# The weights' rounding on GpSimd, row sums ended once per pair, and three units' activations rounded on ScalarE

## The chip, the core and the metric

The kernel runs on one core of one Trainium2 chip. The metric is device time in microseconds: the median before is 724.19 us over three runs (723.75 to 724.37). Five engines work on the core, each through its own instructions in order: TensorE (PE, with its weight loads as PEld), VectorE (DVE), ScalarE (ACT), GpSimd (POOL) and SyncE (SP, which issues nearly all transfers). Semaphores tie them together.

## The reference

Sliding-window attention with a few sink tokens, whose output goes through a two-layer network with a clipped activation:

```
scores = q @ k.T / sqrt(64)              # 4 batches, 8 heads, 768 tokens, 64 wide
keep   = (pos_k < 4) | ((0 <= i - j) & (i - j < 128))
a      = softmax(where(keep, scores, -1e9))
x      = (a @ v) as 3072 tokens x 512
h      = x @ w_in                        # 512 x 2048, float64 in memory
g      = h * clip(h + 3, 0, 6) / 6
out    = g @ w_out                       # 2048 x 512, float64 in memory
```

## The kernel before

A unit is 256 tokens of one batch; there are 12 (3 for each of 4 batches). The four units that begin a batch come first, then the other eight. For each unit the attention runs in 4 pairs of heads, so there are 48 pairs, `s` = 0 to 47. Pairs 0 to 9 are plain (`plain(s)`): they see no earlier tokens and use unsplit float32 products. Two heads of a pair and two blocks of 128 tokens give four score blocks.

For one plain pair the steps are: scores on PE (`sp`, L309), masked minimum on DVE (L316), exponential on ACT with a row sum into `sm` (L338), for each head on DVE a sum plus 1e-9 (L340) and a reciprocal `rc` (L341), the division of each block by its row sum (`norm`: token block 0 on DVE at L326, block 1 on ACT at L324), transposes on PE (`pt`, L364), a copy to SBUF on ACT (`pf`, L35), the product with V on PE (`av`, L431), and the split of the result into a rounded high part `xh` (ACT, L35) and a low part `xl` (DVE, L447).

The network works in 8 slices `i` of 256 hidden columns (`ffn1`, `ffn2`), each product in three terms of high and low parts. For a unit and a slice PE writes `hps` (L472, 24 products of 256 columns), ACT makes relu(h + 3) in `gf` (L484), DVE clips and multiplies (L485), then `gf` is rounded to `gh` (L41, on DVE) and DVE subtracts to get `g` (L487). PE then runs 12 products of 512 columns (L498), one slice later in units 0 and 1 and two later from unit 2 on.

The weights come as float64 and are turned into a rounded high and a low part once, slice by slice: `wih0` and `wil0`, `woh0` and `wol0`, `wih1` and so on, 16 parts of 128 x 1024. Each part (`load_part`) is a transfer into `st`, an ACT pass into `wt` (L157), an ACT pass on `st` (L161), two DVE passes (L163, L165) that end in the float32 value in `wt`, a rounding copy to the high part (ACT, L35) and a DVE subtraction for the low part (L168). Three buffers serve `st` and two serve `wt`, so a part can only start when an older one is through. The parts are asked for in pairs 2 to 10, one to three per pair (`WN`).

What each engine does next is fixed at build time. The code is written as a software pipeline (`ORDER`), in which a pair's scores, its softmax and its product with V stand in three successive rounds and steps of the network fill the places between them, and a scheduler then sets each engine's order. In pairs 0 to 3 PE also runs products whose result nobody uses (`idle`, L81). The letters in `WHI`, `GHI` and the like choose the engine: D is DVE, A is ACT, P is POOL. `eng(which, s)` takes the letters after the first for units 0 to 2 (it is called with 4 times the unit's number, and `START` is 9) and the first letter from unit 3 on.

Of the kernel before, what the change touches and what calls it, by code (L numbers as in the profile page):

```python
# [14 lines left out]
ALU = mybir.AluOpType  # L15
# [3 lines left out]
P = 128  # L19
# [7 lines left out]
def split_parts(nc, hi, lo, src, hi_engine, lo_engine):  # L27

    copy_r(nc, hi_engine, hi, src)
    lo_engine.tensor_tensor(out=lo, in0=src, in1=hi.bitcast(F32), op=ALU.subtract)  # L30


def copy_r(nc, eng, out, src, scale=1.0):
    if eng is nc.scalar:
        nc.scalar.mul(out=out, in_=src, mul=scale)  # L35
    elif eng is nc.gpsimd:
        nc.gpsimd.tensor_scalar(out=out, in0=src, scalar1=scale, scalar2=1.0, op0=ALU.mult, op1=ALU.mult)
    elif scale != 1.0:
        nc.vector.tensor_scalar(out=out, in0=src, scalar1=scale, scalar2=None, op0=ALU.mult)
    else:  # L40
        nc.vector.tensor_copy(out=out, in_=src)  # L41
# [3 lines left out]
def attn_ffn_kernel(ctx: ExitStack, tc: tile.TileContext, qx, kx, vx, vfx, vsx, n_sink, window, w_in, w_out, out):  # L45
    nc = tc.nc
# [3 lines left out]
    H, D, UT = 2 * NP, 64, 256  # L50
# [26 lines left out]
    def keep_busy(n):  # L77

        idle = ps.tile([P, 512], F32, tag="bank", name="idle")
        for _ in range(n):  # L80
# [15 lines left out]
                                   op0=ALU.mult, op1=ALU.add)  # L96
# [30 lines left out]
    WOH = [const.tile([P, 2, DM], F32R, name=f"woh{i}") for i in range(NFP)]  # L127
    WOL = [const.tile([P, 2, DM], F32R, name=f"wol{i}") for i in range(NFP)]
    wide = mybir.dt.size(w_in.dtype) == 8
    WHI, WLO = "A", "D"  # L130

    def weng(which, at):
        return {"D": nc.vector, "P": nc.gpsimd, "A": nc.scalar}[which[at % len(which)]]
# [5 lines left out]
    def load_part(hi, lo, src, rows, at):  # L139

        def like(t):
            return t.rearrange("p (a b) -> p a b", a=rows)

        st = work.tile([P, PW, 2], I32, tag=("sb0", "sb1", "K")[at % 3 if at < LAST else at % 2], name="st", bufs=1)
        if not wide:
            st = like(st.rearrange("p n w -> p (n w)").bitcast(F32)[:, 0:PW])
            nc.sync.dma_start(out=st, in_=src)
            split_parts(nc, hi, lo, st, nc.scalar, nc.vector)
            return

        it = work.tile([P, PW], I32, tag=("w0", "kt")[at % 2 if at < LAST else 0], name="wt", bufs=1)
        nc.sync.dma_start(out=like(st.rearrange("p n w -> p (n w)")), in_=src.bitcast(I32))
        low, high = st[:, :, 0], st[:, :, 1]
        ft = it.bitcast(F32)


        nc.scalar.activation(out=ft, in_=high.bitcast(F32), func=AF.Abs, scale=2.0 ** -112)  # L157

        nc.scalar.activation(out=low, in_=low.bitcast(U32), func=AF.Copy, scale=2.0 ** -29 * (1 - 2.0 ** -18),  # L161
                             bias=7.5 * 2.0 ** -18 - 0.5)
        nc.vector.scalar_tensor_tensor(out=low, in0=high, scalar=-2 ** 31, in1=low,  # L163
                                       op0=ALU.bitwise_and, op1=ALU.bitwise_or)
        nc.vector.scalar_tensor_tensor(out=it, in0=it, scalar=3, in1=low,  # L165
                                       op0=ALU.logical_shift_left, op1=ALU.bitwise_or)
        copy_r(nc, weng(WHI, at), hi, like(ft))
        weng(WLO, at).tensor_tensor(out=lo, in0=like(ft), in1=hi.bitcast(F32), op=ALU.subtract)  # L168
# [31 lines left out]

    SSE = "DD"
    START = 9
    GHI, GLO = "DD", "DD"
    XHI, XLO = "DDA", "DD"
    KHI, KLO, QHI, QLO = "AA", "DD", "AA", "DD"

# [18 lines left out]
    def plain(s):  # L225
        return s < NF32 and pus[s][1] == 0
# [62 lines left out]
    def cell(s, h, t, c0, c1):  # L289

        if plain(s):
            return st_[s][f"P{h}"][:, t * P + c0:t * P + c1]
        return st_[s]["P"][:, h, t * WP + c0:t * WP + c1]
# [26 lines left out]
    NORM0, NORM = "DADA", "AAAA"  # L320

    def norm(e, blk, c):
        if e == "A":
            nc.scalar.mul(out=blk, in_=blk, mul=c)  # L324
        elif e == "D":
            nc.vector.tensor_scalar(out=blk, in0=blk, scalar1=c, scalar2=None, op0=ALU.mult)  # L326
        else:
            nc.gpsimd.tensor_scalar(out=blk, in0=blk, scalar1=c, scalar2=1.0, op0=ALU.mult, op1=ALU.mult)

    def C_soft(s, h):  # L330
        b, u, p = pus[s]
        d = st_[s]
        nb, sm, rc = d["nb"], d["sm"], d["rc"]
        hs = slice(2 * h, 2 * h + 2)
        live = [(0, W2), (0, W2)] if u else [(0, P), (0, 2 * P)]
        for t in range(2):
            i, blk = 2 * h + t, cell(s, h, t, *live[t])
            d["exp"] = nc.scalar.activation(out=blk, in_=blk, func=AF.Exp, scale=-1.0,  # L338
                                            bias=nb[:, i:i + 1], accum_out=sm[:, i:i + 1])
        nc.vector.tensor_scalar(out=sm[:, hs], in0=sm[:, hs], scalar1=1e-9, scalar2=None, op0=ALU.add)  # L340
        nc.vector.reciprocal(out=rc[:, hs], in_=sm[:, hs])  # L341
        if u:

            both = d["P"][:, h].rearrange("p (t w) -> p t w", t=2)[:, :, P:2 * P]
            prior = d["P"][:, h, 0:2 * WP].rearrange("p (t w) -> p t w", t=2)[:, :, 0:P]
            nc.gpsimd.tensor_tensor(out=both, in0=both, in1=prior, op=ALU.add)  # L346
            live = [(P, W2), (P, W2)]
        for t in range(2):
            i, blk = 2 * h + t, cell(s, h, t, *live[t])
            norm((NORM0 if s < START else NORM)[i], blk, rc[:, i:i + 1])  # L350
        if u and h == 1:

            ss = ssc.rearrange("p (t k h y) -> p t k h y", t=2, k=2, h=2)
            snk_in = d["P"][:, :, 2 * P:2 * WP].rearrange(
                "p h (t y) -> p t h y", t=2)[:, :, :, 0:SK]
            split_parts(nc, ss[:, :, 0], ss[:, :, 1], snk_in, weng(SSE, 0), weng(SSE, 1))

    def D_pt(s, h):
        b, u, p = pus[s]
        d = st_[s]  # L360
        blocks = ((0, P), (1, P + SK)) if u else ((0, 0), (1, 0), (1, P))
        pt = ps.tile([P, 512], F32, tag="bank", name="pt")
        for j, (t, c) in enumerate(blocks):
            nc.tensor.transpose(out=pt[:, j * P:(j + 1) * P], in_=cell(s, h, t, c, c + P), identity=ident)  # L364
        w = P * len(blocks)
        if plain(s):
            ph = work.tile([P, 512], F32, tag="ph", name="pf")
            copy_r(nc, {"D": nc.vector, "A": nc.scalar}[PFE[h]], ph[:, 0:w], pt[:, 0:w])
            d[f"pt{h}"] = ph
            return  # L370
        ph = work.tile([P, 512], F32R, name="ph")
        pl = work.tile([P, 512], F32R, name="pl")
        d[f"pt{h}"] = (ph, pl)
        if not u:
            split_parts(nc, ph[:, 0:w], pl[:, 0:w], pt[:, 0:w], nc.scalar, nc.vector)
            return


        own, prior = ([x.rearrange("p (t s q) -> p t s q", t=2, s=2)[:, :, i, :] for x in (ph, pl)] for i in (1, 0))
        split_parts(nc, own[0], own[1], pt[:, 0:w].rearrange("p (t q) -> p t q", t=2), nc.scalar, nc.vector)  # L380
        for i in range(2):
            nc.gpsimd.affine_select(out=prior[i], in_=own[i], pattern=[[0, 2], [-1, P]], base=0,  # L382
                                    channel_multiplier=1, compare_op=ALU.is_gt, fill=0.0)
            nc.gpsimd.affine_select(out=own[i], in_=own[i], pattern=[[0, 2], [1, P]], base=0,
                                    channel_multiplier=-1, compare_op=ALU.is_ge, fill=0.0)
# [174 lines left out]
    def slot_C(s, h, t):  # L560
        if 0 <= s < NS:
            C_score(s, h, t)
            if t == 1:
                C_soft(s, h)
                if s == 0 and h == 1:
                    keep_busy(WARM[1])
                elif 0 < s < NP:
                    keep_busy(WARM[2])
# [62 lines left out]
    with tc.If(flag == 1):  # L631
        with ExitStack() as gen:
# [71 lines left out]
            with tc.For_i(0, B, 1) as bi:  # L704
                for u in range(NU):
                    xn = gp.tile([P, NP, UT], F32, name="xn")
                    for c in range(NP):
                        nc.sync.dma_start(out=xn[:, c, :],
                                          in_=xv[ds(bi, 1), :, c, u * UT:(u + 1) * UT].rearrange("o p s -> (o p) s"))
# [75 lines left out]
```

## Time and profile before

| | |
|---|---|
| median of 3 runs | 724.19 us |
| the profiled execution: its time, and the span of its records | 723.47 us, 721.8 us |
| PE busy | 706.4 us, 98% |
| DVE busy | 497.0 us, 69% |
| ACT busy | 420.6 us, 58% |
| POOL busy | 173.2 us, 24% |
| TensorE clock granted, mean over the span | 0.994 |

The span is what the records cover; the run's own time is 1.7 us longer. PE counts as busy while a product is in its pipeline, so short gaps between products are hidden in "busy". An idle stretch is put down to the instruction that ended it. The shares are means over stages that differ much: the first 110 us, in which the weights are prepared, look unlike the rest.

### The profile page before, as it was taken

What the parts mean: (1) busy time and instruction counts of PE and PEld (TensorE: products, weight loads), DVE (VectorE), ACT (ScalarE), POOL (GpSimd) and SP (SyncE); (2) the same over time, 40 slices, a digit from 0 to 9 for tenths busy, and PEclk for the clock granted to TensorE, in tenths of its full rate; (3) what the DMA queues carried; (4) which work ended last, traced back from release to release, by engine and by line L of the source; (5) the groups of instructions that cost most, each with busy time, mean ns of one, the idle gap of its engine ahead of it and who ended that gap; (6) DMA issues with size and microseconds to landing.
All of it is one profiled execution on the core that took longest, in us unless ns stands there. A gap on an engine that the chain in (4) does not pass through costs nothing. (4 is left out here: it accounts for less than half of the span.)

```text
span 721.8 us, 14212 instructions
## 1 busy us (share of the span) xinstructions
PE 706.4 (98%) x4772; PEld 638.3 (88%) x4772; DVE 497.0 (69%) x1370; ACT 420.6 (58%) x1091; POOL 173.2 (24%) x336
## 2 busy tenths in 40 slices
PE   9898899999999999999999999999999999999996
PEld 7776788999999999999998998999999999998985
DVE  5799888657676776777777777777777677543331
ACT  5999777556566556566566665655665665411211
POOL 1000000000035334325334434343334335200000
PEclk9999899999999999999999999999999999999999
DMA  7667555344454454555544544553644632000000
GB/s 290 201 209 242 189 173 156 89 103 134 109 139 132 126 134 132 135 139 137 138 118 118 161 115 115 136 147 90 182 119 109 170 93 61 30 1 1 30 1 34
DMA packets 53296, 89.10 MB, mean 123 GB/s; under 512 B 8160, under 2 KB 38112, under 8 KB 51168
## 3 DMA queue, kind: packets, MB, share of 16 engines
q1 hardware_dynamic: 53072, 88.11, 43.6%
q8 instruction: 40, 0.66, 0.4%
q14 instruction: 40, 0.33, 0.2%
q10 hardware_dynamic: 144, 0.00, 0.0%
HBM read 42.47 MB, written 6.29 MB: 68 GB/s over the span
## 5 line engine op out<-in xcount | busy, mean ns | idle before, releaser
L472 PE MATMUL hps<-xh,wih 128*128 128x256 f32 x768 | 220.7, 287 | 4.0 <-ACT wih L35 4.0
L472 PE MATMUL hps<-xh,wil 128*128 128x256 f32 x768 | 218.0, 284 | 0.7 <-DVE wil L168 0.7
L472 PE MATMUL hps<-xl,wih 128*128 128x256 f32 x768 | 217.0, 282 | 1.2 <-DVE xl L447 1.2
L498 PE MATMUL o<-woh,gh 128*128 128x512 f32 x384 | 155.0, 404 | 0.6 <-DVE gh L41 0.6
L472 PEld LDWEIGHTS hps<-xh,wih 128*128 128x128 f32 x768 | 145.6, 190 | 7.3 <-ACT wih L35 5.3
L498 PE MATMUL o<-wol,gh 128*128 128x512 f32 x384 | 151.7, 395 | 0.0
L498 PE MATMUL o<-woh,g 128*128 128x512 f32 x384 | 151.5, 395 | 0.0
L472 PEld LDWEIGHTS hps<-xl,wih 128*128 128x128 f32 x768 | 145.7, 190 | 2.4 <-DVE xl L447 1.4
L472 PEld LDWEIGHTS hps<-xh,wil 128*128 128x128 f32 x768 | 145.6, 190 | 1.7 <-DVE wil L168 1.1
L485 DVE SCALAR_TENSOR_TENSOR gf<-gf,hps 128x512 f32<-128x512 f32 x96 | 65.8, 685 | 83.1 <-ACT gf L484 82.2
L346 POOL TENSOR_TENSOR Pt<-Pt 128x256 f32<-128x256 f32 x64 | 47.4, 741 | 295.8 <-ACT Pt L338 295.7
L338 ACT ACTIVATE Pt<-Pt,nb 128x272 f32<-128x272 f32 (+2 forms) x152 | 77.0, 507 | 66.8 <-DVE nb L316 65.9
L484 ACT ACTIVATE gf<-hps,three 128x512 f32<-128x512 f32 x96 | 66.0, 687 | 81.9 <-PE hps L472 80.9
L324 ACT ACTIVATE Pt<-Pt,rc 128x144 f32<-128x144 f32 (+2 forms) x152 | 55.7, 414 | 65.3 <-DVE rc L341 41.8
L498 PEld LDWEIGHTS o<-woh,g 128*128 128x128 f32 x384 | 72.2, 188 | 16.7
L498 PEld LDWEIGHTS o<-woh,gh 128*128 128x128 f32 x384 | 72.4, 189 | 11.0 <-DVE gh L41 1.0
L498 PEld LDWEIGHTS o<-wol,gh 128*128 128x128 f32 x384 | 72.5, 189 | 10.0
L487 DVE TENSOR_TENSOR g<-gf,gh 128x512 fp32r<-128x512 f32 x96 | 69.7, 726 | 0.7
L316 DVE CUSTOM_DVE_ANT_0 Pt<-sp,m_t 128x272 f32<-128x272 f32 x128 | 54.0, 429 | 12.0 <-PE sp L314 10.7
L314 PE MATMUL sp<-K 128*128 128x272 f32 (+2 forms) x304 | 60.7, 285 | 0.0
L382 POOL TENSOR_SCALAR_AFFINE_SELECT ph<-ph 128x256 fp32r<-128x256 f32 x64 | 30.8, 480 | 119.0 <-ACT ph L35 119.0
L314 PEld LDWEIGHTS sp<-K 128*128 128x128 f32 x304 | 51.2, 188 | 6.4
(96 smaller groups left out, 1086.3 us busy)
## 6 DMA issues: line engine op xcount, KB each, us to landing
K<-kt SPq DMA_DIRECT2D x128, 200.0 KB, 3.5
K<-kt SPq DMA_DIRECT2D x152, 64.0 KB, 2.1
st<-in_w_in_dram SPq DMA_DIRECT2D x8, 1024.0 KB, 5.3
st<-in_w_out_dram SPq DMA_DIRECT2D x8, 1024.0 KB, 5.0
kr<-in_kx_dram SPq DMA_DIRECT2D x32, 200.0 KB, 2.4
qr<-in_qx_dram SPq DMA_DIRECT2D x48, 128.0 KB, 2.3
out_dram<-ost SPq DMA_DIRECT2D x24, 256.0 KB, 2.4
vr<-in_vx_dram SPq DMA_DIRECT2D x32, 192.0 KB, 2.5
```

The costliest lines, as they stand in the source:

```text
L314: nc.tensor.matmul(out=sp[:, 0:w], lhsT=Q[:, h, t * P:(t + 1) * P], rhs=K[:, h, part, k0c:k0c + w], start=(part == 0), stop=(part == 1))
L316: d["min"] = nc.vector.tensor_tensor_reduce(out=cell(s, h, t, 0, w), in0=sp[:, 0:w], in1=m[:, 0:w], scale=-SCALE, scalar=3.0e38, op0=ALU.a ...
L324: nc.scalar.mul(out=blk, in_=blk, mul=c)
L338: d["exp"] = nc.scalar.activation(out=blk, in_=blk, func=AF.Exp, scale=-1.0, bias=nb[:, i:i + 1], accum_out=sm[:, i:i + 1])
L346: nc.gpsimd.tensor_tensor(out=both, in0=both, in1=prior, op=ALU.add)
L382: nc.gpsimd.affine_select(out=prior[i], in_=own[i], pattern=[[0, 2], [-1, P]], base=0, channel_multiplier=1, compare_op=ALU.is_gt, fill=0.0)
L472: nc.tensor.matmul(out=hp[:, half, :], lhsT=l, rhs=r, start=(j == 0), stop=(j == n - 1))
L484: nc.scalar.activation(out=gf, in_=hp, func=AF.Relu, bias=three, scale=1.0)
L485: nc.vector.scalar_tensor_tensor(out=gf, in0=gf, scalar=6.0, in1=hp, op0=ALU.min, op1=ALU.mult)
L487: eng(GLO, state["n"] * NP).tensor_tensor(out=g, in0=gf, in1=gh.bitcast(F32), op=ALU.subtract)
L498: nc.tensor.matmul(out=acc, lhsT=l[:, f, ts_], rhs=r[i][:, f, :], start=(i == 0 and f == 0 and j == 0), stop=(i == NFP - 1 and f == 1 and ...
```

## The change

`WHI` becomes "P": the rounding of all 16 weight parts moves from ACT to POOL, and `copy_r` uses a plain copy there in place of a multiplication by two scalars. `GHI` becomes "DA": for units 0, 1 and 2 the rounding of `gf` to `gh`, 24 instructions, moves from DVE to ACT. In plain pairs (0 to 9) the sum plus 1e-9 and the reciprocal are done once for both heads on four columns, after the second head's exponentials, and the divisions of both heads follow.

```
@@ copy_r
     elif eng is nc.gpsimd:
-        nc.gpsimd.tensor_scalar(out=out, in0=src, scalar1=scale, scalar2=1.0, op0=ALU.mult, op1=ALU.mult)
+        nc.gpsimd.tensor_copy(out=out, in_=src)
@@ attn_ffn_kernel
-    WHI, WLO = "A", "D"
+    WHI, WLO = "P", "D"
...
-    GHI, GLO = "DD", "DD"
+    GHI, GLO = "DA", "DD"
@@ C_soft, behind the exponentials of head h
+        heads = [h]
+        if plain(s):
+            if h == 0:
+                return
+            heads, hs = [0, 1], slice(0, 4)
         nc.vector.tensor_scalar(out=sm[:, hs], in0=sm[:, hs], scalar1=1e-9, scalar2=None, op0=ALU.add)
         nc.vector.reciprocal(out=rc[:, hs], in_=sm[:, hs])
...
-        for t in range(2):
-            i, blk = 2 * h + t, cell(s, h, t, *live[t])
-            norm((NORM0 if s < START else NORM)[i], blk, rc[:, i:i + 1])
+        for g in heads:
+            for t in range(2):
+                i, blk = 2 * g + t, cell(s, g, t, *live[t])
+                norm((NORM0 if s < START else NORM)[i], blk, rc[:, i:i + 1])
```

The scheduler builds a new order on PE, DVE and ACT for the first 110 us or so. Six lines are added ahead of most of the code, so a line of after is 6 higher from L351 on and L340, L341 become L345, L346. Three places follow.

First place, DVE around slice 1 and the low part `wil1` (the numbers behind names are buffers; `wt_509` of before is `wt_499` of after). Before:

```order
L163 SCALAR_TENSOR_TENSOR st_508<-st_508 128x1024
L165 SCALAR_TENSOR_TENSOR wt_509<-wt_509,st_508 128x1024
L168 TENSOR_TENSOR wil1_120<-wt_500,wih1_112 128x1024
L485 SCALAR_TENSOR_TENSOR gf_531<-gf_531,hps_486 128x512
L168 TENSOR_TENSOR wol1_136<-wt_509,woh1_128 128x1024
L41 CAST gh_530<-gf_531 128x512
```

After:

```order
L168 TENSOR_TENSOR wil1_120<-wt_490,wih1_112 128x1024
L326 TENSOR_SCALAR Ph_439<-Ph_439,rc_438 128x128
L326 TENSOR_SCALAR Ph_448<-Ph_448,rc_438 128x128
L165 SCALAR_TENSOR_TENSOR wt_499<-wt_499,st_498 128x1024
L163 SCALAR_TENSOR_TENSOR st_626<-st_626 128x1024
L168 TENSOR_TENSOR wol1_136<-wt_499,woh1_128 128x1024
L491 SCALAR_TENSOR_TENSOR gf_521<-gf_521,hps_476 128x512
L165 SCALAR_TENSOR_TENSOR wt_627<-wt_627,st_626 128x1024
L493 TENSOR_TENSOR g_519<-gf_521,gh_520 128x512
```

`wil1` moved ahead of the last pass on `woh1`, only one pass now stands between that pass and `wol1`, which reads POOL's rounding, and `gf` stands behind `wol1`.

Second place, DVE around `wol4` and `wil5`. Before:

```order
L165 SCALAR_TENSOR_TENSOR wt_884<-wt_884,st_883 128x1024
L163 SCALAR_TENSOR_TENSOR st_892<-st_892 128x1024
L163 SCALAR_TENSOR_TENSOR st_1045<-st_1045 128x1024
L168 TENSOR_TENSOR wol4_139<-wt_884,woh4_131 128x1024
L165 SCALAR_TENSOR_TENSOR wt_893<-wt_893,st_892 128x1024
```

After:

```order
L326 TENSOR_SCALAR Ph_830<-Ph_830,rc_814 128x128
L165 SCALAR_TENSOR_TENSOR wt_868<-wt_868,st_867 128x1024
L165 SCALAR_TENSOR_TENSOR wt_877<-wt_877,st_876 128x1024
L168 TENSOR_TENSOR wol4_139<-wt_868,woh4_131 128x1024
L168 TENSOR_TENSOR wil5_124<-wt_877,wih5_116 128x1024
L491 SCALAR_TENSOR_TENSOR gf_918<-gf_918,hps_885 128x512
```

Two last passes and the two low parts that need POOL's roundings now stand in a row.

Third place, ACT between slice 3's `gf` of unit 0 and the copies that follow. Before:

```order
L484 ACTIVATE gf_807<-hps_774,three_75 128x512
L161 ACTIVATE st_883<-st_883 128x1024
L324 ACTIVATE Ph_829<-Ph_829,rc_828 128x256
L338 ACTIVATE Ph_848,sm_827<-Ph_848,nb_826 128x256
L35 ACTIVATE xh2_870<-av_861 128x256
L35 ACTIVATE wih4_115<-wt_875 128x1024
```

After:

```order
L490 ACTIVATE gf_793<-hps_760,three_75 128x512
L324 ACTIVATE Ph_699<-Ph_699,rc_698 128x256
L324 ACTIVATE Ph_714<-Ph_714,rc_698 128x256
L161 ACTIVATE st_867<-st_867 128x1024
L35 ACTIVATE pf_777<-pt_773 128x384
L35 ACTIVATE pf_802<-pt_798 128x384
L157 ACTIVATE wt_868<-st_867 128x1024
L35 ACTIVATE gh_792<-gf_793 128x512
```

The rounding of `wih4` is gone from ACT, and the new rounding `gh_792` stands six instructions behind its `gf`.

## Rows read from the trace of the kernel before

**Rows 1.** Busy time by stretch of the span: length, then busy us (and instructions) of PE, PEld, DVE, ACT and POOL, the granted clock, the DMA share and GB/s.

```profile
30.00:40.00 10.00, 7.84 (x52) 6.30 (x52) 8.96 (x25) 9.94 (x22) 0.00 (x0) 1.00 0.79 263
40.00:80.00 40.00, 36.32 (x212) 28.75 (x212) 38.68 (x80) 36.88 (x68) 0.00 (x0) 1.00 0.68 230
80.00:90.00 10.00, 8.38 (x35) 7.24 (x36) 8.19 (x21) 7.23 (x15) 0.00 (x0) 0.66 0.39 134
90.00:110.00 20.00, 20.00 (x129) 17.33 (x127) 16.96 (x34) 16.21 (x32) 0.00 (x0) 1.00 0.52 165
110.00:200.00 90.00, 90.00 (x616) 82.08 (x615) 61.88 (x188) 57.28 (x153) 1.47 (x2) 1.00 0.46 121
200.00:650.00 450.00, 450.00 (x3152) 414.39 (x3151) 324.01 (x921) 261.88 (x737) 168.62 (x318) 1.00 0.46 119
```

**Rows 2.** All waits of PE over the span: who waited for whom, us in total, times, the longest.

```profile
PE hps L472 <- ACT wih L35: 4.0, 3, 2.1
PE pt L364 <- DVE Ph L326: 1.6, 1, 1.6
PE idle L81 <- POOL rel L65: 1.2, 1, 1.2
PE hps L472 <- DVE xl L447: 1.2, 1, 1.2
PE hps L472 <- DVE wil L168: 0.7, 1, 0.7
PE o L498 <- DVE gh L41: 0.6, 1, 0.6
```

**Rows 3.** Busy time by stretch again, behind the wait for slice 5; the granted clock is the third number from the end.

```profile
81.00:82.00 1.00, 0.39 (x2) 0.30 (x2) 1.00 (x5) 1.00 (x4) 0.00 (x0) 0.94 0.54 82
82.00:85.00 3.00, 3.00 (x9) 2.03 (x9) 3.00 (x9) 3.00 (x7) 0.00 (x0) 0.50 0.87 334
85.00:88.00 3.00, 3.00 (x16) 3.00 (x16) 3.00 (x8) 1.55 (x3) 0.00 (x0) 0.50 0.25 81
88.00:89.00 1.00, 1.00 (x7) 1.00 (x7) 0.19 (x1) 0.00 (x0) 0.00 (x0) 0.65 0.00 0
```

**Rows 4.** Groups of instructions of the first 130 us by line, engine and shape: count, busy us and mean ns of one, idle time before them.

```profile
L165 DVE SCALAR_TENSOR_TENSOR wt<-wt,st 128x1024 int32<-128x1024 int32 x16 | 19.5, 1217 | 0.1
...
L168 DVE TENSOR_TENSOR wol<-wt,woh 128x1024 fp32r<-128x1024 f32 x8 | 9.8, 1222 | 0.6 <-ACT woh L35 0.6
...
L35 ACT ACTIVATE woh<-wt 128x1024 fp32r<-128x1024 f32 x8 | 8.5, 1063 | 0.5 <-DVE wt L165 0.5
L35 ACT ACTIVATE wih<-wt 128x1024 fp32r<-128x1024 f32 x8 | 8.4, 1052 | 0.2 <-DVE wt L165 0.2
...
L487 DVE TENSOR_TENSOR g<-gf,gh 128x512 fp32r<-128x512 f32 x11 | 7.5, 683 | 0.0
...
L41 DVE CAST gh<-gf 128x512 fp32r<-128x512 f32 x11 | 4.6, 421 | 0.7 <-PE o L498 0.7
...
L340 DVE TENSOR_SCALAR sm<-sm 128x2 f32<-128x2 f32 x23 | 3.5, 163 | 0.4 <-ACT Ph L338 0.2
L341 DVE RECIPROCAL rc<-sm 128x2 f32<-128x2 f32 x23 | 3.4, 157 | 0.2
...
L35 ACT ACTIVATE vs<-raw_s 128x512 fp32r<-128x512 f32 x2 | 1.2, 620 | 0.0
```

**Rows 5.** The same view for POOL over the whole span: the copies, and a two-input instruction.

```profile
L346 POOL TENSOR_TENSOR Pt<-Pt 128x256 f32<-128x256 f32 x64 | 47.4, 741 | 295.8 <-ACT Pt L338 295.7
...
L72 POOL CAST ident_r<-ident 128x128 fp32r<-128x128 f32 x1 | 0.3, 292 | 0.1
...
L188 POOL COPY m_t<-m_t 128x16 bf16<-128x16 bf16 x1 | 0.2, 196 | 0.0
```

**Rows 6.** Timeline of DVE at 194 and 291 us: start us, us, instruction; a number in brackets is the idle time before it.

```profile
194.42 0.99 DVE L41 CAST gh<-gf 128x512 fp32r<-128x512 f32 x1
...
291.39 0.43 DVE L41 CAST gh<-gf 128x512 fp32r<-128x512 f32 x1
...
291.85 1.25 DVE L487 TENSOR_TENSOR g<-gf,gh 128x512 fp32r<-128x512 f32 x1
```

**Rows 7.** Timeline of POOL at the same two places.

```profile
194.40 0.73 POOL L346 TENSOR_TENSOR Pt<-Pt 128x256 f32<-128x256 f32 x1 [185.76 <-ACT Pt L338]
...
291.82 0.74 POOL L346 TENSOR_TENSOR Pt<-Pt 128x256 f32<-128x256 f32 x1 [3.13 <-ACT Pt L338]
```

**Rows 8.** Timeline of DVE at the low parts of slices 1 and 5, and behind the latter.

```profile
39.79 1.22 DVE L168 TENSOR_TENSOR wil<-wt,wih 128x1024 fp32r<-128x1024 f32 x1
...
81.59 1.23 DVE L168 TENSOR_TENSOR wil<-wt,wih 128x1024 fp32r<-128x1024 f32 x1
...
90.04 0.69 DVE L485 SCALAR_TENSOR_TENSOR gf<-gf,hps 128x512 f32<-128x512 f32 x1 [1.85 <-ACT gf L484]
...
92.05 0.42 DVE L447 TENSOR_TENSOR xl<-av,xh 128x256 fp32r<-128x256 f32 x1 [0.79 <-ACT xh L35]
```

**Rows 9.** All waits of DVE between 40 and 82 us.

```profile
DVE wol L168 <- ACT woh L35: 0.6, 2, 0.3
DVE gf L485 <- ACT gf L484: 0.3, 1, 0.3
DVE Ph L316 <- PE sp L309: 0.2, 1, 0.2
```

## The prediction, made before the run

> **What bounds the kernel now.** I read the time by stretches first. From 110 us on PE is busy without a gap (90.00 of 90, 450.00 of 450), DVE and ACT have a quarter to two fifths of their time free [rows 1]. Nothing that only makes an engine lighter there can move the end; time can be won or lost only as long as PE waits, in the first 110 us. There the picture is turned round: between 40 and 80 us DVE is busy 38.68 of 40 us and ACT 36.88 of 40, while PE shows gaps [rows 1]. Both are preparing weights. POOL does nothing in that time.
>
> The list of PE's waits says what those gaps are worth: three waits for a high part of w_in, 4.0 us; one each for a normalised block, 1.6, for `xl`, 1.2, for `wil`, 0.7, for `gh`, 0.6 [rows 2]. (The 1.2 us for `rel` is the program's start.) That is 8.1 us. Beside the waits stands the clock: it falls to 0.50 (1.2 GHz in place of 2.4) at about 82 us, right behind PE's longest wait of 2.1 us, and is back before 89 [rows 2, 3]. The stretch from 80 to 90 us has a mean of 0.66 [rows 1], so 3.4 us of work at full speed are lost. 8.1 + 3.4 = 11.5 us is what a faster preparation could give at the very most.
>
> The question is therefore what the change does to the pace of DVE, the fuller of the two, from the first weight to the last. In the ledger below I count from the low part of slice 1 (39.79 us) to that of slice 5 (81.59) [rows 8], 41.8 us in which DVE waits only 1.1 us [rows 9]. The sum is made against the profiled run (723.47 us with a span of 721.8); it lies 0.7 us under the median of 724.19, and I put the difference that comes out on the median.
>
> **Prices.** A high part on ACT is 1.05 to 1.06 us [rows 4]; 16 of them, 16.9 us, leave ACT. On POOL no copy of that size is in the trace. Its CAST of 128 columns takes 292 ns and its COPY of 16 columns 196 ns [rows 5]: 0.86 ns a column, so 292 + 896 x 0.86 = 1.06 us by this estimate. The upper bound is the two-input instruction, 741 ns for 256 columns [rows 5], 2.96 us for 1024; I take 1.06, since the CAST is the same operation, and a copy has one input. `gh` on ACT is priced by the nearest copy of 128x512, 620 ns [rows 4]; on DVE it took 421 [rows 4]. One sum and one reciprocal fewer per plain pair is 163 + 157 = 0.32 us of DVE [rows 4].
>
> **Term 1, up to the first slices: -1.4 us.** Three roundings (`wih0`, `woh0`, `wih1`) leave ACT ahead of the first network steps, at most 3.2 us. Against that, a block of head 0 is now normalised only when head 1's exponentials are through. In the order of ACT a weight pass (L157 or L161) mostly stands in that place, so it costs little. Bounds: -3.2, all of ACT's time on the path, and +1.6, PE's one wait for a normalised block [rows 2] a second time. I take -1.4, a little on the side of the gain, because three of the first four pairs have such a pass there. PE's waits for a normalised block and `xl` (2.8 us together) are those that it can shorten.
>
> **Term 2, slice 1 to slice 5: +1.1 us.** Removed from DVE: four `gh`, 4 x 0.42 = 1.7; three pairs' ends, 3 x 0.32 = 1.0; the waits of 1.1 us, nearly all for ACT, 1.0. Added: DVE and POOL collide. Alone, `g` takes 683 ns; where POOL had begun a tensor-tensor 0.03 us before it, it took 1.25 us, and `gh`, 421 ns alone, took 0.99 [rows 4, 6, 7]. Both ended 0.28 to 0.54 us after POOL did, so DVE stood still while POOL worked. The passes L163, L165, L168 and L487 all take two inputs from SBUF, as that `g` does. Eight roundings (`woh1`, `wih2`, ... `wih5`) fall in the ledger. For three of them, `woh1`, `woh2`, `woh4`, the order leaves DVE nothing to do but a further weight pass and then the low part that needs POOL's result: the full 1.06 each, 3.2 us. `wih2` and `wih4` come when DVE has work from PSUM or waits for ACT anyway: nothing, and if that cover were gone, 2.1. For `woh3`, `wih3` and `wih5` it is a toss-up which engine comes first, 0 to 3.2, I take 1.6. So -1.7 - 1.0 - 1.0 + 3.2 + 1.6 = +1.1, bounds -3.7 (no collision) and +4.8 (all eight).
>
> The Trainium skill has a rule that speaks against this move (SBUF — State Buffer, Who interferes with whom): the port pair that VectorE and GpSimd share is an exclusive lock, and a VectorE instruction with two SBUF inputs and a GpSimd instruction that reads SBUF fully block each other, the second to issue waiting for the whole of the first. By that rule in full, every one of the eight costs DVE 1.06 us and the term is +4.8. The trace agrees in kind (1.25 us in place of 0.683), but shows no copy of this length.
>
> **Term 3, slice 5 to about 100 us: -1.5 us.** Here DVE waited 1.85 us for ACT's `gf` and 0.79 for `xh` [rows 8], since PE ran at half speed. Work that is late can fill most of that, 2.1 us. Two `gh` (0.8) and two pair ends (0.6) leave DVE, two roundings (`woh5`, `wih6`) come in, 2.1. -2.1 - 0.8 - 0.6 + 2.1 = -1.4, rounded with the smaller POOL share to -1.5. The wait for slice 5 stays by term 2, so I expect the clock to fall again; if it doesn't, up to 3.4 us more are won, if it falls twice, 3.4 are lost.
>
> **Terms at nothing.** 13 of the 24 `gh` and the last slices' roundings come after 100 us. 13 x 0.62 = 8 us go to an ACT that has 57.28 of 90 us busy [rows 1]. Without that cover each `gh` would come later by the difference of the two prices, 13 x 0.20 = 2.6 us. The scores' minimum, which reads PSUM, stays where it was. No transfer is added or moved past another, but buffers for `st` and `wt` come free when DVE is through, so transfers follow DVE's pace.
>
> **The sum.** -1.4 + 1.1 - 1.5 = -1.8 us: 724.2 - 1.8 = 722.4.
>
> **Rivals.** Three, beside the forecast.
>
> *Slower: POOL stops DVE every time.* All 14 roundings between 28 and 110 us cost DVE their 1.06 us, 14.8 us. DVE saves 11 `gh` (4.6) and 10 pair ends (3.2), and can give up about half of the 7.2 us that it was idle from 30 to 110 (8.96 + 38.68 + 8.19 + 16.96 = 72.8 of 80 us busy, [rows 1]). 14.8 - 4.6 - 3.2 - 3.6 = +3.4, and 0.6 more for the `gh` that DVE now waits for: +4.0, 728.2. For it: DVE at 38.68 of 40, and the two collisions. Against it: DVE often has a PSUM instruction next. It decides as soon as the collisions in the ledger cost more than 6.6 us in place of 4.8. Its chance is 0.27. The Trainium skill's rule above, taken in full, is this rival's mechanism; no run here shows it yet for copies of this length.
>
> *Faster: no collision to speak of.* The order happens to give DVE other work whenever POOL runs, or copies don't collide as sums do. Term 2 becomes -3.7: -1.4 - 3.7 - 1.5 = -6.6, 717.6. For it: all waits of PE [rows 2] are for things that come earlier then. Against it: the three places in the order where nothing else can be done. 0.15.
>
> *No change: ACT's rounding is a new wait.* `gf`, ACT, DVE, ACT, DVE is one more crossing for each slice, and ACT's order puts six instructions between `gf` and `gh` in slice 3 (two norms, two passes, two copies: 2 x 0.4 + 2 x 1.05 + 2 x 0.38, 3.7 us by estimate). Slices where ACT has this queue cost PE up to 2 us, once or twice: -1.8 + 1.8 = 0, 724.2. The change then only shifts the waits. 0.27.
>
> **How the numbers follow.** The forecast, a gain of 1.5 to 4 us, gets 0.31. Under 0.2% (1.45 us) either way, about what a measurement of this kernel can tell from no change, gets 0.27. Faster is 0.31 + 0.15 = 0.46, slower 0.27. The range goes to the fast rival below (717.5) and a little past the slow one above (728.5), which leaves out 0.07 and 0.10.
>
> **What will show it.** POOL's copies of 128x1024 near 1.06 us, or longer where DVE holds them up (term 2). DVE's L163, L165 and L168 with means above 1.22 us, or idle time put down to POOL, about 5 us up to slice 5. `wil1` ready near 39.5 us in place of 41.0 (term 1), `wil5` within 1.5 us of 82.8. PE's waits for `wih` put down to POOL, at slices 4 to 6, and the clock at half once between 75 and 92 us. PE without gaps from 112 us. I am wrong if PE's waits sum to less than 4 us or more than 14, if the clock falls twice, or if the time after 110 us is no longer the same as before.

## The result, and the profile after

The changed kernel takes 731.85 us (median of 4 runs, 730.77 to 732.43), the kernel before beside it 724.28 us (723.75 to 726.12): a ratio of 1.0101, 95% interval 1.008 to 1.0122. It is slower by 7.3 us, where 1.8 us faster was forecast. The profiled execution took 731.42 us with a span of 729.7 us, 7.95 us more than that of before. Single executions of some kernels took far longer (856 to 3923 us): they are in no ratio below, and `no_round`'s profiled one is among them.

The stretches after, with the columns of [rows 1]; the last three lie around the places where the clock was at half:

```profile
30.00:40.00 10.00, 7.55 (x38) 5.64 (x37) 9.96 (x21) 8.60 (x20) 3.02 (x2) 0.83 0.60 197
40.00:80.00 40.00, 36.81 (x206) 29.24 (x206) 33.93 (x65) 30.24 (x60) 8.96 (x6) 0.91 0.60 208
80.00:90.00 10.00, 7.69 (x47) 6.09 (x46) 9.06 (x17) 5.98 (x12) 2.96 (x2) 0.94 0.62 196
90.00:110.00 20.00, 17.64 (x101) 14.78 (x100) 15.36 (x28) 13.10 (x29) 4.07 (x3) 0.95 0.46 169
110.00:200.00 90.00, 89.81 (x608) 80.52 (x607) 60.67 (x169) 64.04 (x162) 2.32 (x2) 1.00 0.47 121
200.00:650.00 450.00, 450.00 (x3155) 414.49 (x3155) 325.08 (x930) 268.92 (x755) 171.06 (x320) 1.00 0.46 121
...
34.00:38.00 4.00, 4.00 (x17) 2.99 (x18) 4.00 (x11) 4.00 (x11) 0.57 (x1) 0.57 0.60 213
48.00:54.00 6.00, 6.00 (x14) 3.64 (x12) 3.17 (x8) 3.75 (x8) 1.10 (x1) 0.50 0.50 175
88.00:92.00 4.00, 3.80 (x20) 3.80 (x21) 3.97 (x13) 3.17 (x9) 0.00 (x0) 0.60 0.82 240
```

From 110 us on nothing has changed but 0.2 us, so the loss lies where the prediction looked. Between 40 and 80 us DVE and ACT are both less busy than before (33.93 and 30.24 us against 38.68 and 36.88, [rows 1]), and PE is no better off: the clock fell there, which it had not done before. All waits of PE, as in [rows 2]:

```profile
PE pt L370 <- DVE Ph L326: 3.7, 4, 1.7
PE hps L478 <- POOL wih L37: 2.0, 2, 1.5
PE o L504 <- ACT gh L35: 1.9, 1, 1.9
PE o L504 <- DVE wol L168: 1.8, 1, 1.8
PE idle L81 <- POOL rel L65: 1.2, 1, 1.2
PE hps L478 <- DVE wil L168: 0.9, 1, 0.9
PE hps L478 <- DVE xl L453: 0.7, 1, 0.7
```

Without the start (`rel`) that is 11.0 us in place of 8.1. The clock lost in the first 130 us (one minus the granted clock, added up over stretches of 2 us) is 6.8 us in place of 3.4. Together 17.8 against 11.5 us, so 6.3 of the 7.95 us are seen as waits or as a slow clock.

Next the weight passes and what POOL stretches, DVE's groups of the first 130 us [rows 4]:

```profile
L163 DVE SCALAR_TENSOR_TENSOR st<-st 128x1024 int32<-128x1024 int32 x16 | 20.0, 1252 | 0.7 <-ACT st L161 0.7
...
L168 DVE TENSOR_TENSOR wol<-wt,woh 128x1024 fp32r<-128x1024 f32 x8 | 11.4, 1420 | 3.8 <-POOL woh L37 3.8
L168 DVE TENSOR_TENSOR wil<-wt,wih 128x1024 fp32r<-128x1024 f32 x8 | 9.7, 1212 | 0.9 <-POOL wih L37 0.9
...
L493 DVE TENSOR_TENSOR g<-gf,gh 128x512 fp32r<-128x512 f32 x9 | 7.0, 779 | 0.2 <-ACT gh L35 0.2
...
L326 DVE TENSOR_SCALAR Ph<-Ph,rc 128x128 f32<-128x128 f32 x18 | 5.6, 355 | 0.1
...
L345 DVE TENSOR_SCALAR sm<-sm 128x4 f32<-128x4 f32 x10 | 2.5, 249 | 1.7 <-ACT Ph L338 1.7
```

How that comes about stands in the timelines of POOL and DVE around slices 1 and 5 (start, length, idle time ahead in brackets). POOL:

```profile
31.20 1.04 POOL L37 CAST woh<-wt 128x1024 fp32r<-128x1024 f32 x1 [13.36 <-DVE wt L165]
...
42.54 1.99 POOL L37 CAST woh<-wt 128x1024 fp32r<-128x1024 f32 x1 [3.13 <-DVE wt L165]
...
82.98 1.98 POOL L37 CAST woh<-wt 128x1024 fp32r<-128x1024 f32 x1 [5.83 <-DVE wt L165]
84.90 1.04 POOL L37 CAST wih<-wt 128x1024 fp32r<-128x1024 f32 x1
```

DVE:

```profile
31.26 1.26 DVE L326 TENSOR_SCALAR Ph<-Ph,rc 128x128 f32<-128x128 f32 x2
...
42.40 1.22 DVE L163 SCALAR_TENSOR_TENSOR st<-st 128x1024 int32<-128x1024 int32 x1
44.56 1.23 DVE L168 TENSOR_TENSOR wol<-wt,woh 128x1024 fp32r<-128x1024 f32 x1 [0.95 <-POOL woh L37]
...
54.90 0.29 DVE L316 CUSTOM_DVE_ANT_0 Ph<-sp,m 128x128 f32<-128x128 f32 x1 [3.03 <-PE sp L309]
...
84.99 2.02 DVE L168 TENSOR_TENSOR wol<-wt,woh 128x1024 fp32r<-128x1024 f32 x1 [0.94 <-POOL woh L37]
86.93 1.21 DVE L168 TENSOR_TENSOR wil<-wt,wih 128x1024 fp32r<-128x1024 f32 x1
```

A copy alone takes 1.04 us. The one at 42.54 began 0.14 us behind DVE's L163 and took 1.99: it stood until DVE had finished, then ran, and DVE waited 0.95 us for it. At 84.90 POOL came 0.09 us first, and DVE's `wol` stood for 0.8 us. At these places whichever is second stands still, and from 84.05 to 87.0 us, beside the second half of one copy and the whole of the next, DVE gets one pass done.

The Trainium skill (SBUF — State Buffer, Who interferes with whom) says just this: the pair of ports is an exclusive lock, and who issues first decides who blocks. The trace agrees, with 1.98 to 1.99 and 2.02 us in place of 1.04 and 1.22; in `dummy_copy` below one copy shows a case that this order of issue does not explain.

### The profile page after: what moved, and what is told of

Same layout as the page of the kernel before. It is cut to its first block, busy times and chain, and to the rows that moved or that the text cites. A ratio compares the mean times of both kernels' runs of the same rounds, so it can differ in the third digit from the quotient of the medians.

```text
span 729.7 us, 14200 instructions
## 1 busy us (share of the span) xinstructions
PE 711.5 (98%) x4772; PEld 639.8 (88%) x4772; DVE 493.0 (68%) x1326; ACT 420.9 (58%) x1099; POOL 196.5 (27%) x352
## 5 line engine op out<-in xcount | busy, mean ns | idle before, releaser
L351 POOL TENSOR_TENSOR Pt<-Pt 128x256 f32<-128x256 f32 x64 | 47.5, 742 | 188.1 <-ACT Pt L338 188.0
L504 PEld LDWEIGHTS o<-wol,gh 128*128 128x128 f32 x384 | 72.9, 190 | 12.3 <-DVE wol L168 2.2
L316 DVE CUSTOM_DVE_ANT_0 Pt<-sp,m_t 128x272 f32<-128x272 f32 x128 | 54.2, 430 | 13.2 <-PE sp L314 11.8
```

The lines of the kernel that those rows point to most:

```text
L316: d["min"] = nc.vector.tensor_tensor_reduce(out=cell(s, h, t, 0, w), in0=sp[:, 0:w], in1=m[:, 0:w], scale=-SCALE, scalar=3.0e38, op0=ALU.a ...
L504: nc.tensor.matmul(out=acc, lhsT=l[:, f, ts_], rhs=r[i][:, f, :], start=(i == 0 and f == 0 and j == 0), stop=(i == NFP - 1 and f == 1 and ...
```

## The experiments

Three theories of the loss stood against each other. A: POOL's copies and DVE's passes stop each other. B: ending the row sums once per pair delays the divisions of head 0, PE waits for them, and its gaps let the clock fall. C: `gh` on ACT is the new wait.

The runs were timed beside the kernel before on the same chip. The columns: ratio to the kernel before with its interval; PE's waits without `rel` and the clock lost up to 130 us, both worked out as above; the profiled execution's time less the 723.47 us of before; and what POOL costs DVE up to 130 us: the sum over DVE's groups of count times (mean less the mean of before), plus DVE's waits for POOL. Only shapes that before has too are in that sum; the rows of kernels without work for POOL (0.3 to 0.6) show how much of it is chance.

| kernel | ratio | waits + clock, us | profiled, us | DVE stretched + waits for POOL, us |
|---|---|---|---|---|
| before | 1 | 8.1 + 3.4 | 0 | 0 |
| changed | 1.0101 [1.008, 1.0122] | 11.0 + 6.8 | +7.95 | 4.2 + 4.7 |
| p_only | 1.0116 [1.0092, 1.0139] | 16.2 + 5.1 | +10.8 | 7.4 + 4.7 |
| r_only | 1.0018 [1.0001, 1.0034] | 10.9 + 8.5 | +6.2 | 0.3 + 0 |
| g_only | 0.9981 [0.9963, 0.9999] | 6.8 + 3.4 | -0.8 | 0.6 + 0 |
| pg | 1.0061 [1.004, 1.0082] | 12.9 + 3.4 | +5.8 | 5.4 + 4.4 |
| pr | 1.0093 [1.0068, 1.0118] | 13.8 + 5.1 | +9.3 | 4.4 + 3.7 |
| gr | 1.0016 [1.0002, 1.003] | 8.2 + 5.1 | +0.7 | 0.3 + 0 |
| dummy_copy | 1.0078 [1.005, 1.0106] | 9.5 + 8.6 | +6.3 | 4.5 + 0 |
| dummy_set | 1.0024 [1.0005, 1.0043] | 9.9 + 5.1 | +3.5 | 3.7 + 0 |
| no_round | 0.9992 [0.997, 1.0013] | | | |
| norm_a | 1.0084 [1.0055, 1.0114] | 8.8 + 6.8 | +4.9 | 2.6 + 4.3 |
| mix_ap | 1.0007 [0.9992, 1.0022] | 8.0 + 5.1 | +2.2 | 2.9 + 3.3 |
| mix_pa | 1.0017 [1.0001, 1.0032] | 9.7 + 3.4 | +2.9 | 2.4 + 0 |
| early8 | 1.0047 [1.0029, 1.0065] | 12.0 + 3.4 | +4.0 | 2.6 + 1.9 |
| late8 | 1.0036 [1.0024, 1.0049] | 8.8 + 5.1 | +4.1 | 1.8 + 2.8 |
| warm2 | 1.013 [1.0104, 1.0156] | 11.6 + 1.7 | +11.8 | 4.5 + 4.3 |
| split4 | 1.0107 [1.0083, 1.0131] | 12.3 + 5.1 | +8.6 | 1.7 + 9.5 |
| g_pa | 1.0037 [1.002, 1.0055] | 9.5 + 8.5 | +7.9 | 3.4 + 1.8 |
| g_ap | 1.0029 [1.0012, 1.0047] | 8.2 + 8.5 | +4.6 | 2.3 + 2.5 |

Waits and clock together, less the 11.5 us of before, give the profiled time within 2 us in every row but split4 (2.7) and warm2 (which runs more products). So they are the right account of a single execution; how often the clock falls differs from one to the next, which is why a profiled time can lie some us off the median behind the ratio. The scheduler builds an order of its own for nearly every one of these kernels, so a difference of one or two us can be the order's; `dummy_copy` and `dummy_set` alone keep that of before, and `split4` that of the changed kernel.

**One part alone: p_only, r_only, g_only.** Each is the kernel before with one part of the change.

```
p_only:  WHI "A" -> "P", and the plain copy in copy_r
r_only:  the row sums ended once per pair
g_only:  GHI "DD" -> "DA"
```

> Only the weights' rounding moves to POOL; gh stays on DVE, the row sums are ended per head as before. Theory A (POOL's copies and DVE's two-input passes stop each other): most of the loss is here, +3 to +7 us on the kernel before, with L163/L165/L168 means above 1.22 us and POOL copies up to 2 us. Theory B (the later divisions of head 0 hold PE up): -2 to +1 us. Theory C (gh on ACT is the new wait): -2 to +1 us.

> Only the row sums of plain pairs are ended once per pair. Theory A: -1 to +1 us. Theory B (the transposes of head 0 wait for head 1's exponential, PE's gaps let the clock fall): +2 to +6 us, with PE waits for Ph near the 3.7 us of the changed kernel and clock falls ahead of 60 us. Theory C: -1 to +1 us.

> Only gh of units 0 to 2 moves to ACT. Theory A and B: -1 to +1 us. Theory C (the crossing DVE-ACT-DVE is a new wait in the slices where ACT has a queue): +2 to +5 us, PE waits for gh near 2 us.

p_only is 8.4 us slower (0.0116 x 724.2), a little more than the whole change and than the 3 to 7 us of theory A; r_only 1.3 us slower, g_only 1.4 us faster, both near the edge of what is told apart. Theory C falls: alone, the crossing to ACT costs PE one wait of 0.4 us. Of theory B only a rest stands: PE's waits for `Ph` did grow (to 4.5 us), but the medians hardly.

**Two parts: pg, pr, gr.** Each is the changed kernel with one part undone.

> The change without its row sums per pair. If the three parts add up (POOL +8.4, gh -1.4, row sums +1.3 us in the runs of one part): +7 us on before, close to the changed kernel. If the row sums were the cause of the lost clock ahead of 60 us: +3 to +5.

> The change without gh on ACT. If the parts add up: +9 to +10 us on before. If gh on ACT is a new wait once POOL is there (ACT is lighter and DVE later): +5 to +6.

> The change without POOL: the weights' rounding stays on ACT, gh of units 0 to 2 goes to ACT, row sums per pair. If POOL is the whole loss: 0 +-1.5 us against before. If a part of it is the other two together (ACT's queue grows long): +2 to +5.

The parts don't add up: by the ratios `gh` on ACT is worth -1.4 us alone, -4.0 beside POOL's copies and +0.6 beside both other parts. But POOL's part costs in any company: p_only against before +8.4, pg against g_only +5.8, pr against r_only +5.4, the changed kernel against gr +6.2 us. Without POOL the change is 1.2 us slower than before. pg has no more clock lost than before and still loses 4.4 us, so the clock is not what the loss needs.

Theory B keeps a share, though. pg came out as its second expectation had it (+3 to +5): without the row sums per pair, 2.9 us of the changed kernel's loss come back, and its clock falls once, between 82 and 90 us, and not ahead of 60. The two intervals just touch, and pr against p_only (-1.7 us) has the row sums on the gaining side, so the size of this share is not shown. pr, at 6.7 us, lies between its two expectations.

**Copies that nobody uses: dummy_copy and dummy_set.** The kernel before, its order on PE, DVE and ACT unchanged row by row, with an instruction of POOL behind L165 for the parts 0 to 13 (`dead` is `WOL[7]`, written over by the last part; dummy_set copies one column, so that the memset comes at the same time):

```
dummy_copy:
+        if at < LAST:
+            nc.gpsimd.tensor_copy(out=like(dead), in_=like(ft))
dummy_set:
+        if at < LAST:
+            nc.gpsimd.tensor_copy(out=dead[:, 0:1], in_=ft[:, 0:1])
+            nc.gpsimd.memset(dead.bitcast(F32), 0.0)
```

> The kernel before, plus 14 copies of 128x1024 on POOL (weight parts 0 to 13), each behind the last pass L165 on the part, into a tile whose content is written over later; nothing waits for what they write, and the order of PE, DVE and ACT is that of the kernel before, row by row. Theory A: DVE loses 0.5 to 1 us per copy in the stretch from 30 to 110 us, +4 to +10 us on the total. Theory B or C (POOL's copies are harmless): within 1 us of before, DVE means unchanged.

> As the run with 14 unused copies on POOL behind L165, but each copy is one column (which sets the time) and then a memset of 128x1024, which writes SBUF and reads none. The order of PE, DVE and ACT is that of the kernel before. If POOL's reading is what stops DVE (or DVE's reading what stops POOL): within 1.5 us of before, DVE means at 1.22, memsets that never stretch. If any use of SBUF by POOL does: +4 to +6 us, as with the copies (ratio 1.0078).

The copies cost 5.6 us though nothing waits for their results and ACT and DVE do all that they did. (One ACT pass waited 0.8 us until a copy had read its `wt`.) DVE's groups in dummy_copy (two lines are added, so L168 is L170, L326 is L328, L340 is L342), with POOL's behind them:

```profile
L165 DVE SCALAR_TENSOR_TENSOR wt<-wt,st 128x1024 int32<-128x1024 int32 x16 | 20.1, 1259 | 0.2
L163 DVE SCALAR_TENSOR_TENSOR st<-st 128x1024 int32<-128x1024 int32 x16 | 19.9, 1247 | 3.3 <-ACT st L161 3.3
L170 DVE TENSOR_TENSOR wol<-wt,woh 128x1024 fp32r<-128x1024 f32 x8 | 10.7, 1337 | 0.1
...
L328 DVE TENSOR_SCALAR Ph<-Ph,rc 128x128 f32<-128x128 f32 x18 | 5.6, 320 | 0.2
L342 DVE TENSOR_SCALAR sm<-sm 128x2 f32<-128x2 f32 x22 | 5.0, 240 | 0.4 <-ACT Ph L340 0.2
...
L168 POOL CAST wol<-wt 128x1024 fp32r<-128x1024 f32 x14 | 22.9, 1633 | 73.7 <-DVE wt L165 40.3 <-DVE sm L342 22.7 <-DVE rc L343 10.6
```

Both sides lose: the copies take 1.63 us on average in place of 1.04, and DVE's passes, the one-input ones among them, are 4.5 us longer in all. In the profiled execution 5.2 of the 6.3 us are lost clock. One copy, begun at 80.43 us, took 5.31 us. The copies (shortest, median and longest in ns), and DVE beside that one:

```profile
L168 POOL CAST wol<-wt x14: 1040/1082/5311, 16.8 to 104.1; 128x1024 fp32r<-128x1024 f32 x14
...
80.22 2.35 DVE L163 SCALAR_TENSOR_TENSOR st<-st 128x1024 int32<-128x1024 int32 x2
82.49 1.21 DVE L170 TENSOR_TENSOR wol<-wt,woh 128x1024 fp32r<-128x1024 f32 x1
83.63 1.21 DVE L165 SCALAR_TENSOR_TENSOR wt<-wt,st 128x1024 int32<-128x1024 int32 x1
```

Four passes of DVE follow each other without a gap and at full pace, three of them begun after the copy, and the copy ends about its own length behind the last (85.74 against 84.84). So it is not always the one that comes second that stands: here POOL stood until DVE's run of passes was over.

With memsets of 0.95 us (dummy_set, four lines added) it is another picture:

```profile
L165 DVE SCALAR_TENSOR_TENSOR wt<-wt,st 128x1024 int32<-128x1024 int32 x16 | 19.5, 1220 | 0.2
L163 DVE SCALAR_TENSOR_TENSOR st<-st 128x1024 int32<-128x1024 int32 x16 | 19.4, 1219 | 5.0 <-ACT st L161 5.0
L172 DVE TENSOR_TENSOR wol<-wt,woh 128x1024 fp32r<-128x1024 f32 x8 | 9.8, 1222 | 0.5 <-ACT woh L35 0.4
...
L330 DVE TENSOR_SCALAR Ph<-Ph,rc 128x128 f32<-128x128 f32 x18 | 7.2, 431 | 0.2
...
L41 DVE CAST gh<-gf 128x512 fp32r<-128x512 f32 x10 | 5.2, 516 | 0.7 <-PE o L502 0.7
...
L170 POOL MEMSET wol<- 128x1024 f32 x14 | 13.4, 954 | 0.8
```

The passes with two inputs are untouched, the memsets never stretch (the one-column copies ahead of them, which read, do: 0.18 to 2.19 us), and only one-input passes over SBUF (the division, 282 to 431 ns; `gh`, 421 to 516) are held up. The loss is 1.7 us, just outside the 1.5 of its first expectation.

**The rounding left out: no_round.** The changed kernel without the 16 roundings: the high parts are two tiles of zeros, and the low parts then carry the weights.

```
-        copy_r(nc, weng(WHI, at), hi, like(ft))
```

> The changed kernel with the rounding of the weights left out altogether: the high parts are two tiles of zeros for all slices, so the output lacks the weights' high parts; loads, passes L163, L165, L168 and all products stay. If POOL's copies are what costs (theory A, by lock and by DVE's wait for their results): 7 to 10 us under the changed kernel, 722 to 725 us, L168 back at 1.22 us. If the other two parts or the order cost it: 728 to 731 us.

723.7 us by the ratio, 7.9 us under the changed kernel, as theory A had it. (Twelve of its runs took 721.5 to 728.4; there is no profile to read, so L168 at 1.22 us is not shown.) This run says something else as well. Here ACT is rid of 16.9 us, DVE of its `gh` and half its pair ends, and POOL does nothing: all that the change relieves, without POOL's copies. It is worth 0.6 us against before, 2.2 us at the end of the interval, with zero inside it. Part by part, from the ratios: -1.4 us for `gh` (g_only), +1.3 for the row sums (r_only) and -1.7 for ACT's 16.9 us (no_round against gr), each of them near the edge of what can be told. Two things are not tested apart: the order is a new one here too, and two thirds of the products of the network have a factor of zero.

**Where the loss can be hidden: norm_a, mix_ap, mix_pa, early8, late8.** All are the changed kernel with one letter or condition changed.

```
norm_a:  NORM0 "DADA" -> "AAAA"
mix_ap:  WHI "P" -> "AP" (w_out on POOL);   mix_pa:  "PA" (w_in on POOL)
early8:  parts 0 to 7 on POOL;   late8:  parts 8 to 15
```

> The changed kernel with the divisions of token block 0 in pairs 0 to 8 on ACT too. DVE loses 18 x 0.28 us of work and the collisions of these one-input instructions with POOL (1.3 us in the changed kernel). Theory A with DVE as the pace: 3 to 6 us under the changed kernel, 726 to 729. If ACT's queue (theory C) sets the pace: no gain or up to 3 us slower.

> The changed kernel with half the copies: the parts of w_in are rounded by ACT as before, those of w_out by POOL. If each copy costs alike: half of the loss, ratio near 1.005 on before. If the copies of w_out are the dear ones (three DVE waits for woh, L168 of wol at 1420 ns): near the changed kernel, 1.008 to 1.010. If PE's waits for POOL's wih are: near before.

> The opposite half: the parts of w_in on POOL, those of w_out on ACT. If each copy costs alike: 1.005. If the copies of w_out are the dear ones: within 0.3% of before. If PE's waits for POOL's wih (2.0 us in the changed kernel, 6.8 with POOL alone) are: 1.007 to 1.010.

> The changed kernel with only the first 8 weight parts (slices 0 to 3, up to about 74 us) rounded by POOL, the last 8 by ACT. If the dear copies are those of the stretch in which DVE has no idle time (40 to 80 us): 1.006 to 1.010 on before, nearly the changed kernel. If all copies cost alike, or what decides is that two parts in a row go over POOL all the way: about 1.005. If half the copies hide in any case: 1.000 to 1.002.

> The other half: slices 0 to 3 by ACT, slices 4 to 7 by POOL. If the dear copies are those of the full stretch from 40 to 80 us: 1.000 to 1.003. If all cost alike: about 1.005. If the copies of slices 4 and 5 (wol4 with 0.94 us of wait and 2.02 us of length at 85 us) are the dear ones: 1.006 or more.

norm_a missed: 5 us less work on DVE brought 1.2 us, within the two intervals. But its 18 divisions went to ACT, where one takes 0.39 us (7.1 us in all), and PE now waits 3.8 us for ACT's divisions in place of 3.7 for DVE's, so it is no test of DVE's relief alone. early8 and late8 halve the loss (3.4 and 2.6 us), so the copies of the fullest stretch are no dearer than others. Taken in turn with ACT, half the copies cost 0.5 and 1.2 us; against gr, the same kernel without POOL, that is nothing (-0.7 and +0.1), where all 16 cost 6.2. Neither run came out at the 1.005 of copies that cost alike. In mix_pa there is a visible reason: DVE never waits for POOL there, since the order has other work behind each L165 of w_in. For mix_ap, with 6.2 us taken from DVE, the table gives none.

**The length of a copy, and the clock: split4, warm2.**

```
split4:  each rounding on POOL as four copies of 256 columns
warm2:   two idle products (L81) behind each softmax of pairs 4 to 8 as well
```

> The changed kernel with each rounding on POOL cut into four copies of 256 columns (the order of the other engines is the same). If DVE stands still for one whole copy and no more: stretched DVE passes lose at most 0.45 us each in place of 1.04, but POOL stands behind a DVE pass up to four times, so its results come later: PE's and DVE's waits for POOL grow, 2 to 6 us above the changed kernel. If the loss goes by DVE's stretched passes alone: 2 to 4 us under it. If by POOL's time in all: within 1 us.

> The changed kernel with two unused products behind each head's softmax in pairs 4 to 8 as well (20 products, about 4 us of TensorE at full speed). If the lost clock is a cause of its own: falls ahead of 60 us vanish, 2 to 4 us under the changed kernel. If it only follows the waits (TensorE is slow while it would have waited anyway): 0 to 4 us above the changed kernel.

split4 is as slow as the changed kernel, as its third expectation had it; the loss only changes its shape. DVE's stretched time falls from 4.2 to 1.7 us, its waits for POOL grow from 4.7 to 9.5:

```profile
DVE wol L170 <- POOL woh L39: 5.7, 5, 1.3
...
DVE wil L170 <- POOL wih L39: 3.8, 5, 1.3
```

warm2 gets 5.1 of the 6.8 us of lost clock back and is 2 us slower than the changed kernel: 20 products are added, two at a time in some 0.5 us, and new waits come up, 3.0 us of them for `K`. A clock kept up by such products costs what it brings here.

**A better version: g_pa, g_ap.** g_only with half the copies on POOL, row sums per head.

> gh of units 0 to 2 on ACT, the w_in parts rounded by POOL and the w_out parts by ACT, row sums ended per head as before. If ACT's relief is worth time as long as DVE's added time is hidden (2.4 us in the run with row sums per pair): 2 to 4 us under before, 0.995 to 0.997, and under gh alone (0.9981). If ACT isn't the bound: 0.998 to 1.002.

> The same with the w_out parts on POOL and the w_in parts on ACT. If ACT's relief counts: 0.995 to 0.998; if DVE's waits for POOL's woh (3.3 us with row sums per pair) eat it, or ACT isn't the bound: 0.999 to 1.003.

Both are 2 to 3 us slower than before and about 4 slower than g_only; g_pa is outside both of its ranges, g_ap inside its second. ACT's relief does not pay for half the collisions. No kernel here beats before by more than g_only's 1.4 us.

## Why the prediction was wrong

**The prices were right.** POOL's copy was put at 1.06 us and takes 1.04 alone; `gh` on ACT at 620 ns and takes 622. The ledger of term 2 can be read again from the two traces, from `wil1` to `wil5`, by the columns of [rows 1]. Before:

```profile
39.79:81.59 41.80, 36.53 (x214) 28.84 (x212) 40.48 (x85) 38.68 (x70) 0.00 (x0) 1.00 0.66 224
```

After, with all waits of DVE in it:

```profile
39.76:86.90 47.14, 42.46 (x239) 33.70 (x240) 40.14 (x73) 33.93 (x66) 11.92 (x8) 0.93 0.61 212
```

```profile
DVE Ph L316 <- PE sp L309: 3.7, 2, 3.0
DVE wol L168 <- POOL woh L37: 2.8, 3, 0.9
DVE xl L453 <- ACT xh L35: 0.3, 1, 0.3
```

The collisions were put at 3.2 + 1.6 = 4.8 us. Measured in the ledger: 2.8 us of waits for `woh`, in three places (those of `woh1`, `woh2` and `woh4`, as forecast), 1.6 for stretched `wol` (4 x 1.62 against 4 x 1.22) and 0.6 for stretched L163 (7 x 1.297 against 1.214): 5.0 us. (The ledger of before holds five `gh` passes, 2.07 us, where the term counted four.) The prediction looked only at passes with two inputs; the one-input ones, which POOL stops too (L326 and L345 above), add 2 us over the first 130 us (18 x (355 - 282) and 10 x (249 - 163) ns), outside the ledger.

**The step that failed: term 2 took DVE as the pace of the ledger and put its wait for PE at nothing.** The term came to +1.1; the ledger grew by 47.14 - 41.80 = 5.34, above its upper bound of 4.8. The parts of DVE's time say where. Its busy time is nearly the same (40.14 and 40.48): some 2.5 us of work are gone, where the term had 2.7 for `gh` and pair ends, and 2.2 us of stretching have come. Its waits for ACT fell from 0.9 [rows 9] to 0.3, where the term had 1.0 gone. 2.8 us of waits for POOL came, inside the 4.8 of the collisions. But its waits for PE's scores rose from 0.2 [rows 9] to 3.7. These 3.5 us, which no term holds, are most of the 4.2 by which the term was short.

3.03 of them stand at one place, and the trace shows the chain that ends there (DVE, ACT and PE, from the timelines):

```profile
45.70 0.68 DVE L491 SCALAR_TENSOR_TENSOR gf<-gf,hps 128x512 f32<-128x512 f32 x1
...
45.82 1.13 ACT L157 ACTIVATE wt<-st 128x1024 f32<-128x1024 f32 x1 [1.12 <-DVE wol L168]
46.85 0.62 ACT L35 ACTIVATE gh<-gf 128x512 fp32r<-128x512 f32 x1
...
47.52 0.56 PE L504 MATMUL o<-woh,gh 128*128 128x512 f32 x1 [1.86 <-ACT gh L35]
```

POOL's copy for `woh1` stands behind L163 and ends at 44.53 in place of about 43.6. DVE's `wol1` waits for it and runs from 44.56 to 45.79; it frees a buffer `wt`, for which ACT's next pass L157 has waited 1.12 us, and in the new order `gf` comes behind it. `gh` stands behind that L157 on ACT, PE waits 1.86 us for `gh`, its clock is at half from 48 to 54 us, and DVE waits 3.03 us, until 54.90, for the scores that PE runs behind these products. So a stall of DVE went through ACT and PE and came back to DVE as a longer one. Not every such wait is POOL's: in gr DVE waits 2.16 us for scores at 47.85, behind a wait of PE of 2.84 us for a normalised block and a clock at half.

Over the whole kernel the credits were too large as well. The faster rival below, which is the sum without collisions, comes to -6.6 us; no_round, without the copies, has -0.6, at most -2.2. The row sums, a gain in the prediction, cost 1.3 us alone. Term 1 (-1.4) did not come: `wil1` starts at 39.76 in place of 39.79 [rows 8], and PE's waits for `Ph` rose from 1.6 [rows 2] to 3.7. ACT's freed time went into waiting: 6.8 us for DVE's `wol`, which frees the buffer `wt`.

**Term 3** (-1.5) measured 7.95 - 5.34 + 0.03 = +2.6 us, with the wrong sign. In the changed kernel the clock is at half in three places, not one, and more than one was named as a sign of being wrong: two of them, near 34 and 48 us, come ahead of the term's stretch, at places that had a full clock before.

**The rivals.** The slower one named the mechanism that was found, POOL and DVE stopping each other, and its time of 728.2 is 3.6 us short. It did not win by its own sign: the collisions in the ledger cost 5.0 us, not more than 6.6, and still the kernel was slower. It overrated the collisions (14.8 us; DVE lost 8.9 up to 130 us) and set 11.4 us of credits against them, so that its direction was right in part by luck, with two terms too large. The faster rival, no collision at all, was built with no_round, which lacks the copies' own time too: forecast 717.6, measured 723.7. So the credits are too large in the forecast and in both of these. Not all that adds to DVE is paid for, either: mix_ap takes 6.2 us from DVE and costs 0.5, dummy_set takes 3.7 and costs 1.7. The third rival's wait for `gh` came (1.9 us), but g_only shows that the move is harmless without POOL.

**The rest.** PE's waits for POOL's `wih` (2.0 us) came as foretold, and PE's work without gaps from 112 us on but for 0.2 us. `wil5` was ready at 88.1 us, not within 1.5 us of 82.8.

**What stays open.** Why the relief is worth so little over the whole preparation. The chain at 42 to 55 us is one place of one execution; that chains of this kind, through DVE, ACT, PE and the two `wt` buffers, set the pace all the way is not shown. Nor is it shown why mix_ap is nearly free, nor how much of each difference is the new order.

## What to carry to other kernels

An idle POOL is no free engine next to a DVE that works from SBUF to SBUF. Pricing the move as the copy's length taken from DVE, for each copy behind which DVE has no work from PSUM, gave 4.8 us where 5.0 were measured; what such a stall then does to the other engines came on top here and was nearly nothing in mix_ap. Test it with copies that nobody uses in the old order. A busy share of 97% in a ramp doesn't make that engine's load the thing to cut: leave the work out once, and see what the relief is worth, before anything is paid for it. Count costs in full and credits only where a wait of the last engine names them.

## What the runs showed of the hardware

- POOL and DVE stop each other for whole instructions in both directions: a copy of 1.04 us took 1.98 behind a DVE pass, a DVE pass of 1.22 took 2.02 behind a copy, two divisions of together 0.48 took 1.26. A copy can stand behind several passes that follow without a gap: 5.31 us behind four of them.
- POOL memsets, which read nothing, leave DVE's two-input passes alone (1220, 1219, 1222 ns) but hold up one-input passes from SBUF to SBUF (282 to 431 ns). Passes with an input in PSUM were stretched by neither (L316 of 128x256 at 418 to 420 ns in all of them). The Trainium skill (SBUF — State Buffer, Who interferes with whom) has both: a two-input pass contends only with a POOL instruction that reads, a copy, cast or tensor_scalar in a two-port mode with either.
- The clock differs between executions of one kernel: of the runs of the kernel before beside no_round, those with a mean clock of 0.993 to 0.995 took 721.96 to 724.72 us, those with 0.989 to 0.991 took 725.11 to 726.70. A mean clock lower by 0.005 went with about 2.6 us, more than the parts r_only and g_only are; where in these runs the clock was at 1.2 GHz is not shown.
